# Splitting the last weight row of a memory-bound decode kernel in two: halved loads, products and sums at the very end, and one store of eight pieces

## The chip, the cores and the metric

The kernel runs on one core of one Trainium2 chip. The metric is the device time of one execution in microseconds (us). A profiled execution also leaves a trace; its "span" runs from the first to the last recorded instruction and is 1.2 to 1.4 us shorter than the device time. Times to three decimals below are from the trace's records of instructions, semaphores and DMA packets, which are finer than the views that are printed.

## The reference

A decode step: one token attends to 65536 cached positions, then goes through a mixing block with an MLP, and everything is added up into one row of 1024 numbers. Cut to what the change touches:

```python
# x 1x1x1024, k_cache/v_cache 1x4x65536x128, wq 1024x4096, wo 4096x1024,
# w1, w2 1024x1024, w3 1024x3584, w4 3584x1024, all bf16
def reference(...):
    xn = _layernorm(x)
    ...                                   # attention: o (1x4096); mixing block: x1 (1x1024)
    gh = _gelu(_layernorm(x1) @ w3)       # 1 x 3584
    return x + o @ wo + x1 + gh @ w4      # 1 x 1024
```

The last sum is the whole subject. The product with `w4` is done as 28 "rows": row r pairs the column `gh[:, r]` (one value on each of 128 partitions) with a tile of 128 x 1024 weights, 256 KB.

## The kernel before

`w4` is loaded last of all, by four transfers of 17, 7, 3 and 1 rows. TensorE multiplies each row in four column tiles: the columns 0 to 255 of the result are collected on partition 0, 256 to 511 on partition 32, and so on to partition 96. All 28 rows, the residual and the product with `wo` are added up in one PSUM bank. Then VectorE casts that bank to bf16 and SyncE stores it as four pieces of 512 B.

```python
w4_parts = [(0, 17), (17, 7), (24, 3), (27, 1)]          # first row, rows
def w4_dma(i):                                           # issued by SyncE
    r0, nr = w4_parts[i]
    _dma(q_sp, chan("w4%d" % i), lambda e: e.dma_start(out=KV[:, 2, r0 * D:(r0 + nr) * D], in_=rows_src(B_w4, r0, nr)), writes=[b_W4[i]])

def out_rows(items, reads, last=False):
    fns = []
    for lhs, rhs in items:                               # lhs = gh_bf[:, r:r+1], rhs = row r of w4
        for jj in range(4):
            fns.append(lambda e, lhs=lhs, rhs=rhs, jj=jj: e.matmul(
                S_ps[32 * jj:32 * jj + 1, 0, 0:256], lhs, rhs[:, 256 * jj:256 * jj + 256],
                start=False, stop=last, tile_position=(0, 32 * jj), skip_group_check=True))
    _grp(q_pe, fns, reads=reads, writes=[b_OUT], partial=True)

# ... attention, mixing block; then:
resid_rows()                                             # residual, by products with an identity
wo_rows()                                                # o @ wo, moved into the same bank
for i, (r0, nr) in enumerate(w4_parts):
    out_rows([...], [b_W4[i], b_gh], last=(i == len(w4_parts) - 1))
_op(q_dve, lambda e: e.tensor_copy(orow[:, :], OUT), reads=[b_OUT], writes=[b_orow])      # the CAST
ev_out = _dma(q_sp, chan("out"), lambda e: e.dma_start(out=out[0, 0, :].rearrange("(j n) -> j n", j=4), in_=orow[0:97:32, :]), reads=[b_orow])
q_sp.wait_all([ev_out])
```

`_op`, `_grp` and `_dma` put one instruction, a group of products, or a transfer on an engine's list, and work out from `reads` and `writes` which semaphores it has to wait for.

## Time and profile before

| | before |
|---|---|
| device time, median of 3 runs | 400.3 us |
| bytes read | 169.87 MB at 426 GB/s over the span |
| last w4 row landed | 396.560 |
| its product done (semaphore) | 396.912 |
| CAST | 396.935 to 397.360 |
| store issued by SyncE | 397.388 to 398.021 |
| end of the span | 399.081 |

The upper two lines say that the kernel is bound by its stream of bytes. The others are the tail: what still has to happen once the last byte is there. I call the time from the last landing to the end of the span "the tail": 2.521 us here. The prediction shows the lines of the views that these numbers come from.

### The profile page before, as it was taken

How to read it: one execution, taken by the hardware profiler on the slowest of the kernel's cores; microseconds unless marked ns; L12 is line 12 of the kernel's file. 1: busy time of each engine (PE TensorE's matmuls, PEld its weight loads, DVE VectorE, ACT ScalarE, POOL GpSimd, SP SyncE). 2: the span in 40 equal slices, each digit the busy share in tenths (PEclk: the TensorE clock that was granted, in tenths of full speed). 3: DMA queues.
4: the chain of work that ended last, by engine and by line, in shares of the span. 5: the costliest groups of instructions: out<-in, count | busy, mean ns of one | idle time of the engine just before them, and what ended most of it. 6: DMA issues, size and time to landing. Idle time of an engine off the chain costs nothing.

```text
span 399.1 us, 3429 instructions
## 1 busy us (share of the span) xinstructions
PE 168.9 (42%) x1523; PEld 59.0 (15%) x1484; DVE 221.4 (55%) x260; ACT 23.9 (6%) x50; POOL 7.7 (2%) x31
## 2 busy tenths in 40 slices
PE   0034767338033713460357036413541362137394
PEld 0011334012001210110012001101120110012232
DVE  0024222994298549833984597269647952895201
ACT  1000000011001100110011002000100110011000
POOL 5000000000000000000000000000000000000000
PEclk9998568555655665575557555855585558555969
DMA  9999899999999999999999999999999999999995
GB/s 420 420 388 493 383 441 466 447 415 427 420 427 429 434 460 434 434 427 420 434 427 420 466 440 434 421 420 434 427 427 466 434 440 420 420 427 434 418 414 229
DMA packets 3759, 169.97 MB, mean 426 GB/s; under 512 B 548, under 2 KB 552, under 8 KB 808
## 3 DMA queue, kind: packets, MB, share of 16 engines
q1 hardware_dynamic: 3608, 169.87, 98.7%
q8 instruction: 5, 0.08, 0.1%
q10 hardware_dynamic: 144, 0.00, 0.0%
q14 instruction: 2, 0.02, 0.0%
HBM read 169.87 MB, written 0.00 MB: 426 GB/s over the span
## 4 chain that ended last, share of the span: by engine, by line
DMA 59%; DVE 25%; PE 12%; issue 1%; ACT 1%; SPq 1%; POOL 0%
DMA KV<-in_A_k_cache_dram 45%; DVE KV L460 18%; DMA KV<-in_B_w_dram 8%; DMA KV<-in_A_x_dram 6%; PE S_ps L411 3%; PE OT_ps L518 2%; DVE mrow L481 2%; PE M_ps L426 2%; PE S_ps L474 2%; PE S_ps L379 1%; ACT p_sb L496 1%; DVE Yall L395 1%; DVE pT_f L509 1%; DVE pT_f L419 1%; PE PT_ps L505 0%
## 5 line engine op out<-in xcount | busy, mean ns | idle before, releaser
L460 DVE STREAM_TRANSPOSE KV<-KV 128x4096 f32<-128x4096 f32 x32 | 140.3, 4422 | 44.3 <-DMA KV<-in_A_k_cache_dram 44.3
L474 PE MATMUL S_ps<-KV,Ycur 128*32 128x512 bf16 x512 | 60.7, 624 | 132.5 <-DVE KV L460 132.5
L518 PE MATMUL OT_ps<-KV,pT_f 128*32 128x512 bf16 x512 | 47.2, 511 | 4.0 <-issue 3.0
L474 PEld LDWEIGHTS S_ps<-KV,Ycur 128*32 128x32 bf16 x512 | 14.3, 126 | 160.0 <-DVE KV L460 142.4
L496 ACT ACTIVATE p_sb<-S_ps,brun 128x1024 bf16<-128x1024 f32 x16 | 17.8, 1114 | 276.6 <-DVE brun L494 176.1
L509 DVE STREAM_TRANSPOSE pT_f<-PT_ps 128x512 f32<-128x512 f32 x32 | 22.5, 702 | 14.0 <-PE PT_ps L505 14.0
L481 DVE TENSOR_REDUCE mrow<-S_ps 128x1 f32<-128x1024 f32 x16 | 19.3, 1205 | 11.3 <-PE S_ps L474 11.3
L484 PE MATMUL M_ps<-Rm,Lmat 128*128 128x16 bf16 x16 | 3.1, 194 | 38.0 <-DVE Rm L482 38.0
L529 DVE SCALAR_TENSOR_TENSOR O_acc<-O_acc,ff,OT_ps 128x512 f32<-128x512 f32 x12 | 9.0, 748 | 14.7 <-PE OT_ps L518 14.7
L518 PEld LDWEIGHTS OT_ps<-KV,pT_f 128*32 128x32 bf16 x512 | 13.1, 115 | 23.8 <-issue 16.4
L411 PE MATMUL S_ps<-KV 128*32 128x512 bf16 x88 | 12.1, 538 | 2.7 <-DVE KV L359 2.7
L339 DVE CAST KV<-KV 128x8 f32<-128x8 bf16 x1 | 0.2, 172 | 22.2 <-DMA KV<-in_A_x_dram 22.2
L578 PE MATMUL S_ps<-KV,o_bf 128*1 128x512 bf16 x64 | 9.9, 484 | 4.5 <-DMA KV<-in_A_wo_dram 4.5
L505 PE MATMUL PT_ps<-p_sb,permR 128*128 128x512 bf16 x16 | 9.7, 607 | 0.8
L426 PE MATMUL M_ps<-ident_f,pT_f 64*128 64x2 f32 (+2 forms) x32 | 7.9, 373 | 2.5 <-DVE pT_f L419 2.5
L484 PEld LDWEIGHTS M_ps<-Rm,Lmat 128*128 128x128 bf16 x16 | 1.7, 104 | 49.3 <-DVE Rm L482 49.3
L582 DVE COPY pT_f<-S_ps 1x512 f32<-1x512 f32 x1 | 0.7, 679 | 14.4 <-PE S_ps L578 14.4
L426 PEld LDWEIGHTS M_ps<-ident_f,pT_f 64*128 64x128 f32 (+2 forms) x32 | 7.7, 326 | 4.7 <-DVE pT_f L419 3.1
L419 DVE COPY pT_f<-S_ps 64x512 f32<-64x512 f32 (+1 forms) x3 | 2.1, 685 | 10.8 <-PE S_ps L411 10.8
L505 PEld LDWEIGHTS PT_ps<-p_sb,permR 128*128 128x128 bf16 x32 | 3.3, 102 | 27.5 <-ACT p_sb L496 14.7
L364 PE MATMUL M_ps<-KV 8*128 8x8 bf16 x1 | 0.2, 184 | 16.1 <-DVE Dmat_f L363 16.1
L642 POOL MEMSET pT_f<- 64x512 f32 x1 | 0.5, 520 | 312.4 <-PE OT_ps L518 312.4
(88 smaller groups left out, 90.2 us busy)
## 6 DMA issues: line engine op xcount, KB each, us to landing
KV<-in_B_w_dram SPq DMA_DIRECT2D x1, 7168.0 KB, 48.0
KV<-in_B_w_dram SPq DMA_DIRECT2D x1, 4352.0 KB, 27.4
KV<-in_B_w_dram SPq DMA_DIRECT2D x2, 2048.0 KB, 28.3
KV<-in_B_w_dram SPq DMA_DIRECT2D x1, 1792.0 KB, 31.3
KV<-in_B_w_dram SPq DMA_DIRECT2D x1, 768.0 KB, 32.7
KV<-in_B_w_dram SPq DMA_DIRECT2D x1, 256.0 KB, 32.9
KV<-in_A_k_cache_dram SPq DMA_DIRECT2D x8, 46.7
KV<-in_A_v_cache_dram SPq DMA_DIRECT2D x8, 28.1
```

The costliest lines, as they stand in the source:

```text
L411: fns.append(lambda e, j=j, k=k, mv=mv: e.matmul(S_ps[32 * (k % 4):32 * (k % 4) + 32, bank + k // 4, :], vec[:, j:j + 1].broadcast_to([P, ...
L419: _op(q_dve, lambda e, b=b, nb=nb: e.tensor_copy(pT_f[0:32 * nb, b, :], S_ps[0:32 * nb, bank + b, :]), reads=[b_S[bank + b]], writes=[b_pT ...
L426: fns.append(lambda e, b=b, nb=nb, c=c: e.matmul(M_ps[:, c0 + 16 * b + c:c0 + 16 * b + 4 * nb:4], pT_f[0:32 * nb, b, c:512:4], ident_f[0:3 ...
L460: _op(q_dve, lambda e: e.transpose(out=KV32[:, s, o:o + 4096], in_=KV32[:, s, o:o + 4096]), reads=[b_KV[s][sub]], writes=[b_KV[s][sub]], l ...
L474: fns.append(lambda e, we=we, cm=cm, mv=mv: e.matmul(S_ps[32 * cm:32 * cm + 32, n % 4, :], Ycur[:, we, :, :].rearrange("p a g -> p (a g)") ...
L481: _op(q_dve, lambda e: e.reduce_max(mrow[:, k:k + 1], S_ps[:, 2 * k:2 * k + 2, :].rearrange("p b c -> p (b c)"), axis=AX.X), reads=b_S[2 * ...
L496: _op(q_act, lambda e: e.activation(p_sb[:, :, :].rearrange("p b c -> p (b c)"), S_ps[:, 2 * k:2 * k + 2, :].rearrange("p b c -> p (b c)") ...
L505: _op(q_pe, lambda e: e.matmul(PT_ps[:, :], permR[:, :], p_sb[:, n % 2, :], start=True, stop=True), reads=[b_p[n % 2], b_const], writes=[b ...
L509: _op(q_dve, lambda e: e.transpose(out=pT_f[:, n % 2, :], in_=PT_ps[:, :]), reads=[b_PT], writes=[b_pT[n % 2]], loop=True)
L518: fns.append(lambda e, q=q, q4=q4: e.matmul(OT_ps[32 * q4:32 * q4 + 32, g % 2, :], pT_bf[:, n % 2, q, :, 1], KV[:, s, 8192 * sub + 512 * q ...
L529: _op(q_dve, lambda e: e.scalar_tensor_tensor(out=O_acc[:, 0:512], in0=O_acc[:, 0:512], scalar=ff[:, k:k + 1], in1=OT_ps[:, k, :], op0=ALU ...
L578: _grp(q_pe, [lambda e, j=j, jj=jj: e.matmul(S_ps[32 * jj:32 * jj + 1, 1, :], o_bf[:, j:j + 1], KV[:, 0, j * D + 512 * jj:j * D + 512 * (j ...
```

## The change

The tail is a chain of product, cast and store, each of which waits for all of the one before. The change tries to take half of the first two off it: the last row is loaded in two halves of 512 columns; while the second half is on its way the first is multiplied and added. For that everything else (residual, `wo`, rows 0 to 23) is copied to SBUF ahead of time, rows 24 to 27 are collected in two PSUM banks, one for each half, and VectorE adds bank and copy for 128 columns per partition at a time. The columns of each partition are then not contiguous in the result (two runs of 128), so that the store has eight pieces of 256 B. The products of the second half use weights already in TensorE, so their weight loads are left out. Cut to its core:

```diff
-        orow = sb("orow", [P, 256], BF)
+        orow = sb("orow", [P, 2, 128], BF)
...
-        w4_parts = [(0, 17), (17, 7), (24, 3), (27, 1)]
+        w4_parts = [(0, 17 * D), (17 * D, 24 * D), (24 * D, 27 * D), (27 * D, 27 * D + 512), (27 * D + 512, 28 * D)]
...
+        n_bulk = 2
+        b_half = [b_S[2], b_S[3]]
+        ost = pT_f[:, 1, 0:256]
+        b_ost = b_pT[1]
+        def w4_row(r, jj):
+            return KV[:, 2, r * D:(r + 1) * D].rearrange("p (h j n) -> p j h n", h=2, j=4)[:, jj, :, :]
...                            # out_rows(i): as before, for the loads 0 and 1, columns in the new order
+        def out_halves(r, halves, i, first=False, last=False):
+            def mm(e, hf, jj):
+                f = kept_matmul if halves == (1,) else lambda e, *a: e.matmul(*a[:3], start=first, stop=last, tile_position=a[3], skip_group_check=True)
+                return f(e, S_ps[32 * jj:32 * jj + 1, 2 + hf, 0:128], gh_bf[:, r:r + 1], w4_row(r, jj)[:, hf, :], (0, 32 * jj))
+            _grp(q_pe, [lambda e, hf=hf, jj=jj: mm(e, hf, jj) for hf in halves for jj in range(4)],
+                 reads=[b_W4[i], b_gh], writes=[b_half[hf] for hf in halves], partial=not first)
...                            # residual and wo products: columns in the new order, counts unchanged
-        for i, (r0, nr) in enumerate(w4_parts):
-            out_rows(...)
-        _op(q_dve, lambda e: e.tensor_copy(orow[:, :], OUT), reads=[b_OUT], writes=[b_orow])
-        ev_out = _dma(q_sp, ..., out=out[0, 0, :].rearrange("(j n) -> j n", j=4), in_=orow[0:97:32, :]), reads=[b_orow])
+        for i in range(n_bulk):
+            out_rows(i)
+        _op(q_dve, lambda e: e.tensor_copy(ost, S_ps[:, 0, 0:256]), reads=[b_S[0]], writes=[b_ost])
+        for r in range(24, 27):
+            out_halves(r, (0, 1), 2, first=(r == 24))
+        for hf in range(2):
+            out_halves(27, (hf,), 3 + hf, last=True)
+            _op(q_dve, lambda e, hf=hf: e.tensor_tensor(out=orow[:, hf, :], in0=ost[:, 128 * hf:128 * hf + 128], in1=S_ps[:, 2 + hf, 0:128], op=ALU.add),
+                reads=[b_ost, b_half[hf]], writes=[b_orow], partial=(hf == 1))
+        ev_out = _dma(q_sp, ..., out=out[0, 0, :].rearrange("(h j n) -> j h n", h=2, j=4), in_=orow[0:97:32, :, :]), reads=[b_orow])
```

## The prediction

> **What bounds the kernel now.** I read the page from the top: the slices first, then the chain of waits for the last 40 us, then the timeline of the last 10 us, then single rows of instructions for prices.
>
> ```profile
> span 399.1 us, 3429 instructions
> ...
> DMA  9999899999999999999999999999999999999995
> GB/s 420 420 388 493 383 441 466 447 415 427 420 427 429 434 460 434 434 427 420 434 427 420 466 440 434 421 420 434 427 427 466 434 440 420 420 427 434 418 414 229
> ...
> HBM read 169.87 MB, written 0.00 MB: 426 GB/s over the span
> ```
>
> The DMA row is at 9 in every slice but one and the last: the kernel streams 169.87 MB, and 169.87 MB at 426 GB/s is the span. The change moves no byte less, so it can touch only what follows the stream. The chain of waits shows where that begins:
>
> ```profile
> 363.60 0.04 issue
> 363.64 32.91 DMA KV<-in_B_w_dram
> 396.56 0.04 issue
> 396.60 0.31 PE S_ps L566 x4
> 396.91 0.02 issue
> 396.94 0.42 DVE orow L647
> ```
>
> The last w4 row (256 KB) lands at 396.56. All that the change can win lies between there and 399.1: 2.5 us, 0.6% of the time. The timeline says what PE, DVE and SyncE do there and before it:
>
> ```profile
> 390.83 0.61 PE L584 MATMUL S_ps<-pT_f,ident_f 64*1 64x256 f32 x8 [1.40 <-ACT pT_f L583]
> 391.37 1.73 PEld L566 LDWEIGHTS S_ps<-KV,gh_bf 128*1 128x1 bf16 x68 [0.44 <-issue]
> 391.37 2.03 PE L566 MATMUL S_ps<-KV,gh_bf 128*1 128x256 bf16 x68
> ...
> 394.09 0.93 PE L566 MATMUL S_ps<-KV,gh_bf 128*1 128x256 bf16 x28 [0.69 <-DMA KV<-in_B_w_dram]
> ...
> 395.95 0.50 PE L566 MATMUL S_ps<-KV,gh_bf 128*1 128x256 bf16 x12 [0.93 <-DMA KV<-in_B_w_dram]
> ...
> 396.60 0.28 PE L566 MATMUL S_ps<-KV,gh_bf 128*1 128x256 bf16 x4 [0.15 <-DMA KV<-in_B_w_dram]
> 396.94 0.42 DVE L647 CAST orow<-S_ps 128x256 bf16<-128x256 f32 x1 [6.78 <-PE S_ps L566]
> 397.39 0.63 SPq L648 DMA_DIRECT2D out_dram<-orow  x1
> ```
>
> PE waits for a landing ahead of each of the last three groups (0.69, 0.93, 0.15 us), so the matmuls are not the bound and earlier work has slack. The tail is then: last landing 396.56; product done 396.91; CAST 396.94 to 397.36; store issued 397.39 to 398.02; store landed, end 399.08. The store is the largest piece: 1.7 of the 2.5 us, and the change hurries nothing in it.
>
> For the price of the new DVE sum there is a row of the same kind, one operand in PSUM, one in SBUF, 128 elements, and its successor shows the cost of a wait of DVE on itself (374.14 + 0.28 to 374.46, 34 ns in the instruction records):
>
> ```profile
> 374.14 0.28 DVE L546 TENSOR_TENSOR cb_R<-M_ps,maskD 32x128 f32<-32x128 f32 x1 [1.15 <-PE M_ps L543]
> 374.46 0.37 DVE L549 TENSOR_REDUCE cb_o<-cb_R 32x32 f32<-32x128 f32 x1
> ```
>
> **What the Trainium skill says.** "VectorE: DVE Perf Modes", section on the TRN2 errata: a Vector instruction costs a fixed part of about 150 cycles plus one cycle per element for an fp32 tensor_tensor, at 0.96 GHz. The trace agrees on the fixed part: the CAST of 256 took 425 ns, which is (256+152)/0.96; for 128 elements the page gives 290 ns and the trace 279, which I use. "TensorE: Matmul & The Clock Gate", section "Single matmul latency": (398+N)/2.4 ns at full clock. The trace models the 256-wide products at 270 ns, the page's 272; 128 columns fewer are 53 ns fewer. "DMA: Bandwidth & Descriptors", section on why a DMA increments its semaphore by 16: the number of engines is the largest divisor of the slowest dimension. The packet records agree: four packets of 512 B, for four rows. The new pattern's slowest dimension is still 4, so I expect four engines with two pieces each. The same page, "Specifications": under 512 B a transfer becomes a read-modify-write. No row of before shows what a 256 B write costs.
>
> **The change part by part**, in the order of the tail.
>
> 1. Landing of the last piece. The packet records give 80 ns from packet to packet for 2048 B and 235 for 6144 B, so 0.038 ns per byte and about 3 ns per packet (estimate). Each engine carried 8 packets of 2048 B for the last row; now it carries 8 + 8 of 1024 B at about 41 ns. That is 8 x 3 ns plus one more semaphore write (9 ns): the end moves from 396.56 to about 396.59, +0.03. The first half lands 8 x 41 = 0.33 us before, at about 396.25. The fifth issue of 0.43 us by SyncE at 364 is hidden under 15 us of queued wo transfer.
>
> 2. Product. Before: 0.042 us from landing to start, 0.31 to the semaphore, of which the N-dependent part shrinks by 53 ns. Left out weight loads: four loads of one column start within 10 ns of each other beside the matmuls, so at most 0.01. After: 396.59 + 0.04 + 0.26 = 396.89, against 396.91. Gain 0.02 including the loss of step 1.
>
> 3. DVE. The CAST of 425 ns becomes a sum of 279 ns: -0.146. But it waits for two semaphores, PE's and its own, and where an instruction does so in before (the sum over OT_ps at 371.15) a separate wait of 21 ns stands 66 ns ahead of it. So it starts about 0.09 after the product, not 0.02: +0.066. Starts 396.98, ends 397.26, against 397.36. Gain so far 0.10.
>
> 4. The first sum must be gone by then. First half at 396.25 + 0.04, product to 396.55, wait 0.09, sum 396.64 to 396.92, plus 34 ns for DVE's wait on itself: 396.95. That is 0.03 before 396.98, so it fits, just. The 24 matmuls of rows 24 to 26 start at 395.95 in six groups of four of 55 to 65 ns (a 256-wide group took 104 ns: 2.03 less 0.27, over 17 rows), so are streamed by 396.28 to 396.34, which may hold the first half up by 0.05 and the end by 0.02.
>
> 5. The copy of the bulk from PSUM to SBUF, about 425 ns as the CAST, starts at 395.07, when the second group is done, and ends at 395.50, more than 1 us before use: free. The reordered columns in the residual and wo products keep their counts (16, 64 and 4 matmuls) and lie before waits: free.
>
> 6. Store. Issue 0.63 as now: 128 pieces of a w4 load were issued in 0.33 to 0.43 us, so four more pieces cost next to nothing in issue. On the engine one packet of 29 ns becomes two of about 20: +0.01. The write of 256 B pieces is unpriced: I put 0 to 0.1, middle 0.04.
>
> Sum: -0.02 (steps 1 and 2) - 0.08 (step 3) + 0.01 (step 4) + 0.05 (step 6) = about -0.04; I take 400.3 - 0.05 = 400.25 us.
>
> **The rivals.** (a) The intended gain arrives whole: the first half is off the tail, product and sum are halved, the store costs nothing more: -0.12 at most, 400.18. For it speaks the bare 146 ns between the two DVE rows; against it the doubled wait of step 3. (b) The small pieces spoil the store: read-modify-write on HBM, or a slower issue of a pattern with one more dimension. 1.7 us of the tail is the store, so 20% more would give +0.35: 400.6. For it speaks the skill's limit of 512 B and an issue that already takes 0.63 where loads take 0.33; against it that only four engines and 2 KB are concerned. (c) A wait takes the place of the one removed: rows 24 to 26, now twice as many matmuls, or the first sum, end late, and the second sum queues behind: +0.05 to +0.1 on step 4, 400.3 to 400.35. Step 4 has a margin of 0.03 only, so this is likely in part. (d) Stream: in the records of before five DMA engines reach the last row about 1 us after the other eleven, and 16 KB instruction fetches on single engines stall one for 1 us (378.24 to 379.30). If added PE instructions moved a fetch onto a late engine, the end would move by up to 0.6 us (16 KB at 27 GB/s, from 6144 B in 235 ns). Against: PE's instructions are unchanged up to the last two groups, so the fetches should fall where they did.
>
> **Range and chances.** (a) to (c) span 400.18 to 400.6; three runs of before lie within 0.02. With some room for (d), 8 times in 10: 400.0 to 400.5. Over 2% would be 8 us, three times the whole tail: faster 0.005, within 2% 0.985, slower 0.01.
>
> **What would show it.** In the timeline of after: landing of the last half within 0.1 of 396.59; four 128-wide matmuls with no weight load; two sums of about 280 ns, the second starting 0.07 to 0.12 after its product's end or 34 ns after the first sum; a copy at about 395.07; a store issue near 0.63, and about 1.05 us from its end to the end of the span. I am wrong if the store takes over 1.9 us from issue to end, if the last landing moves by over 0.2, or if the second sum starts over 0.1 after both its producers.

## The result

The changed kernel took 400.35 us (median of 6 fast runs, 400.25 to 400.52); the kernel before took 400.3 us in the same rounds (median of 6, 400.28 to 400.65). The ratio is 1.0, with a 95% interval of 0.9987 to 1.0013. Ratios here and below are the mean time of one kernel's fast runs over that of the other's of the same rounds, so not quite the ratio of the medians quoted. The predicted 400.25 us, range and class hold.

A time that doesn't move says nothing of whether the parts did what they should. The page of the changed kernel shows the same stream as before:

```profile
span 398.9 us, 3478 instructions
...
DMA  9999899999999999999999999999999999999995
```

There are 49 instructions more, and not one slice of the DMA row differs. The timeline of the last 4 us (start and duration in us, engine, line, operation, count, and in brackets what ended the idle time ahead of it):

```profile
394.94 0.42 DVE L677 COPY pT_f<-S_ps 128x256 f32<-128x256 f32 x1 [5.94 <-PE S_ps L586]
...
395.85 0.58 PE L593 MATMUL S_ps<-KV,gh_bf 128*1 128x128 bf16 x28 [0.96 <-DMA KV<-in_B_w_dram]
396.54 0.22 PE L562 MATMUL S_ps<-KV,gh_bf 128*1 128x128 bf16 x4
396.55 0.61 DVE L682 TENSOR_TENSOR orow<-pT_f,S_ps 128x128 bf16<-128x128 f32 x2 [1.19 <-PE S_ps L593]
397.20 0.67 SPq L684 DMA_DIRECT2D out_dram<-orow  x1
```

The copy of the bulk sits 0.9 us ahead of the next landing, harmless. The 28 products are rows 24 to 26 and the first half of row 27. The last four products are half as wide as the four before the change, and no line of weight loads goes with them. The two sums follow each other within one group; the store is issued at 397.20 where it was 397.39. The chain of waits says what the end hangs on (start, duration, what):

```profile
363.05 32.76 DMA KV<-in_B_w_dram
...
395.85 0.61 PE S_ps L593 x28
...
396.55 0.30 DVE orow L682
396.85 0.03 issue
396.88 0.29 DVE orow L682
```

It now ends in sum after sum: it holds that the second sum began when the first was over (396.85 + 0.03), not when the second product was done. That is worth a check, because both could be true at once; the experiments take it up.

Step by step, "after" being this profile:

| us | before | after | difference |
|---|---|---|---|
| last landing | 396.560 | 396.501 | |
| landing to product's semaphore | 0.352 | 0.285 | -0.067 |
| product's semaphore to end of CAST, or of the second sum | 0.448 | 0.382 | -0.066 |
| end of that to start of the store's issue | 0.028 | 0.028 | 0 |
| issue | 0.633 | 0.672 | +0.039 |
| end of issue to end of the span | 1.060 | 1.046 | -0.014 |
| tail: last landing to end | 2.521 | 2.413 | -0.108 |

The tail is 0.11 us shorter, and that is 0.03% of 400 us. Against it stands one loss, which lies ahead of the landing: the time from the last landing of rows 24 to 26 to the last landing of row 27 was 0.654 us before and 0.697 after, +0.043. The same bytes come in twice as many packets, which start 42.3 ns apart on the engine that lands last (80.3 ns for packets of double size), and with one more semaphore to write. This count is too kind to the change, because the landing of rows 24 to 26 comes later too; before_again has a better one.

### The profile page after: what moved, and what is told of

Read it like the earlier page. It is cut to its first block, busy times and chain, and to the rows that moved or that the text cites. A ratio compares the mean times of both kernels' runs of the same rounds, so it can differ in the third digit from the quotient of the medians.

```text
span 398.9 us, 3478 instructions
## 1 busy us (share of the span) xinstructions
PE 176.1 (44%) x1555; PEld 59.5 (15%) x1496; DVE 221.9 (56%) x262; ACT 23.9 (6%) x50; POOL 7.7 (2%) x31
## 4 chain that ended last, share of the span: by engine, by line
DMA 58%; DVE 25%; PE 13%; issue 1%; ACT 1%; SPq 0%; POOL 0%; DVEq 0%
DMA KV<-in_A_k_cache_dram 45%; DVE KV L460 18%; DMA KV<-in_B_w_dram 8%; DMA KV<-in_A_x_dram 6%; PE S_ps L411 3%; PE OT_ps L518 2%; DVE mrow L481 2%; PE M_ps L426 2%; PE S_ps L474 2%; PE S_ps L379 1%; ACT p_sb L496 1%; DVE Yall L395 1%; DVE pT_f L509 1%; PE PT_ps L505 1%; DVE pT_f L419 1%
## 5 line engine op out<-in xcount | busy, mean ns | idle before, releaser
L505 PE MATMUL PT_ps<-p_sb,permR 128*128 128x512 bf16 x32 | 18.6, 581 | 0.8
L606 PE MATMUL S_ps<-KV,o_bf 128*1 128x512 bf16 x64 | 8.8, 442 | 4.6 <-DMA KV<-in_A_wo_dram 4.6
```

What stands on the lines that cost most here:

```text
L505: _op(q_pe, lambda e: e.matmul(PT_ps[:, :], permR[:, :], p_sb[:, n % 2, :], start=True, stop=True), reads=[b_p[n % 2], b_const], writes=[b ...
L606: _grp(q_pe, [lambda e, j=j, jj=jj: e.matmul(S_ps[32 * jj:32 * jj + 1, 1, :].rearrange("p (h n) -> p h n", h=2), o_bf[:, j:j + 1], KV[:, 0 ...
```

## The experiments

Theory: every part does what it was made for and the tail is shorter by 0.11 us, of which the split landing takes back 0.05 to 0.08; the rest, 0.03 to 0.06 us, is below what separates two runs of one kernel. Rivals: the shorter tail is a chance of one profile; the store's small pieces eat the gain; a new wait (sum after sum) eats it. The first six runs take these apart; two price the store, three try to use what they showed, and the last looks at a point that had come up on the way.

### after_again: the changed kernel once more, with five rounds

No edit.

> The changed kernel again, unaltered, to see what is stable and what is run-to-run spread. Main theory (the tail after the last landing is about 0.11 us shorter, and that is lost in the spread of whole runs): last landing of w4 to end of span 2.41 us within 0.03 (before: 2.52), the landing itself anywhere within 0.3 us of 396.5, median time within 0.15 us of before, verdict same. Rival (the stream got slower by the finer pieces and ate the gain): the last landing at least 0.1 us later than the 396.56 of before.

The timeline of this second profile, the line of the two sums:

```profile
396.82 0.62 DVE L682 TENSOR_TENSOR orow<-pT_f,S_ps 128x128 bf16<-128x128 f32 x2 [1.18 <-PE S_ps L593]
```

The tail is 2.418 us (2.413 in the first profile), but everything lies 0.27 us later, because the last landing came at 396.769 in place of 396.501. Timed: 400.59 us (median of 5) against 400.51 us for before (median of 9 in the same rounds), ratio 1.0004 (0.999 to 1.0017). So the tail repeats to 0.005 us, and the landing ahead of it moves by more than twice the gain from one execution to the next. The sign that was set for the rival (a landing 0.1 us later than 396.56) came true as well; the next run shows that it proves nothing, since the kernel before moves as far.

### before_again: the same for the kernel before

No edit, one look.

> The kernel before, unaltered, for a second profile of its tail. Main theory: last landing to end of span 2.52 us within 0.03, so the 0.11 us of difference to the changed kernel (2.41, 2.42) is real and not spread; the landing of the last row within 0.3 us of 396.56, so landings scatter by more than the gain. Rival: the tail itself scatters by 0.1 us, and this one gives anything down to 2.42.

The timeline:

```profile
397.17 0.42 DVE L647 CAST orow<-S_ps 128x256 bf16<-128x256 f32 x1 [7.91 <-PE S_ps L566]
397.63 0.63 SPq L648 DMA_DIRECT2D out_dram<-orow  x1
```

Landing 396.799, tail 2.525 us (2.521). The difference of the tails is 0.108 from the first two profiles and 0.107 from the second two: it is not chance. The landings of before (396.56, 396.80) and after (396.50, 396.77) lie in the same band, and a landing that comes 0.27 us later outweighs a tail that is 0.108 us shorter.

What the split costs ahead of the landing is seen best from a mark that the change doesn't touch: the landing of the last block of `v_cache`, near 360 us. From there to the last landing of `w4` it took 36.510 to 36.523 us in the three profiles with whole rows (before, before_again, two_by_two) and 36.582 to 36.604 in the ten that load as the kernel after does (all other runs but adjacent): a loss of 0.075 us. Counted from the landing of rows 24 to 26 it is smaller, 0.642 to 0.654 against 0.694 to 0.711 in nine of the ten (0.668 in one_row). The packet records have the two parts: the packets of the last row take about 0.04 us longer (from the first one's start to that of the semaphore's write, 0.645 us for the whole row, 0.687 to 0.696 for the halves), and from that last packet to the semaphore it takes 0.501 to 0.506 us in place of 0.474 to 0.476 (0.480 in act_load). Why the second part grew no run shows.

From the same mark to the end of the span it is 39.044 and 39.043 us before, 39.004 and 39.013 after. So the whole change gains about 0.035 us: 0.108 in the tail less 0.075 ahead of it.

### one_bank: halved loads and products, but one bank and one CAST

```diff
-        b_half = [b_S[2], b_S[3]]
+        b_half = [b_S[0], b_S[0]]
-   ... S_ps[32 * jj:32 * jj + 1, 2 + hf, 0:128] ...
+   ... S_ps[32 * jj:32 * jj + 1, 0, 128 * hf:128 * hf + 128] ...
-        (copy to ost, two sums)
+        _op(q_dve, lambda e: e.tensor_copy(orow[...], S_ps[:, 0, 0:256]), reads=[b_S[0]], writes=[b_orow])
```

> The load of the last row in two halves, the halved products and the eight-piece store stay; what goes is the second half of the change: all is summed in one PSUM bank and evacuated by one CAST of 256 elements after the last product. Theory of the working (DVE is the piece that gains: 425 ns with one wait becomes 289 ns with two): last landing to end 0.042 + 0.25 + 0.023 + 0.425 + 0.03 + 1.72 = 2.49 us, 0.07 to 0.08 more than the changed kernel. Rival (the gain is the shorter product and the DVE part nothing): 2.42.

The timeline has narrow last products and one wide CAST:

```profile
396.63 0.22 PE L562 MATMUL S_ps<-KV,gh_bf 128*1 128x128 bf16 x4
396.90 0.42 DVE L681 CAST orow<-S_ps 128x256 bf16<-128x256 f32 x1 [7.92 <-PE S_ps L562]
```

Landing 396.593, end 399.082: a tail of 2.489 us, as expected. One time: 400.42 us. With the VectorE part undone, 0.07 to 0.08 of the 0.11 us are gone (2.489 against 2.413 to 2.418); what stays against before, 0.03, is the narrower product less the dearer store. The two banks, the copy and the sums do earn their share.

### reload: the second half's products load their weights again

```diff
-                f = kept_matmul if halves == (1,) else lambda e, *a: e.matmul(...)
+                f = lambda e, *a: e.matmul(...)
```

> The changed kernel, but the second half's four matmuls load their weights again. Theory (weight loads of one column lie beside the matmuls): landing of the last half to the product's semaphore 0.285 us as now, within 0.01. Rival (left-out loads are part of the gain): 0.02 us or more longer.

In the timeline the weight loads of the last four products are back (PEld is TensorE's weight load):

```profile
396.53 0.09 PEld L593 LDWEIGHTS S_ps<-KV,gh_bf 128*1 128x1 bf16 x4 [0.26 <-DMA KV<-in_B_w_dram]
396.53 0.23 PE L593 MATMUL S_ps<-KV,gh_bf 128*1 128x128 bf16 x4
```

From the landing (396.484) to the product's semaphore it took 0.300 us where the kept weights have 0.285: 0.015 us, halfway between the two expectations, so it decides neither. In its record the first product starts as soon after the landing as with kept weights (0.044 against 0.042 us); where the 0.015 us arise, one profile doesn't show. The tail was 2.442 us. The one time, 400.18 us, is the lowest of that call, with the costlier kernel: a reminder of what single times are worth here.

### one_wait: each sum waits for TensorE alone

The first reading of the chain was that the second sum waits for the first. In the kernel after, each sum carries two waits: for the products, and for VectorE itself. Here each half of `orow` has its own bookkeeping, and a tiny memset waits for the bulk copy long before, so that each sum has the one wait that matters.

```diff
+        _op(q_dve, lambda e: e.memset(mrow[:, 0:1], 0.0), reads=[b_ost], writes=[b_mrow[0]])
...
-                reads=[b_ost, b_half[hf]], writes=[b_orow], partial=(hf == 1))
+                reads=[b_ost, b_half[hf]], writes=[b_orow[hf]])
```

> The two sums no longer wait for DVE itself (two separate marks for the halves of the output row, and a tiny memset takes the wait for the copied bulk early), so each waits for PE alone. Theory that the doubled wait costs 66 ns on the path: the second sum starts 0.02 to 0.04 us after its product's semaphore instead of 0.093, last landing to end of span 2.34 us (0.07 less than the changed kernel). Rival (the second sum was held by the first one's end, not by its waits): it starts no earlier against its product than now, 2.41 us. Whole time: not to be told from before, ratio 1.000 within 0.001.

The second sum started 0.024 us after its product's semaphore in place of 0.093. The tail was 2.394 us, not shorter still, because in this profile the last four products ran at a lower granted clock: the trace models them at 263 ns each, not 216, and their semaphore came 0.333 us after the landing, not 0.285. Timed: 400.34 us (median of 5) against 400.51 for before in the same rounds, ratio 0.9994 (0.998 to 1.0008): a lower median than after_again had in the same rounds (400.59), and still not told apart from before. Its five times (400.26 to 400.45) lie almost wholly under the five of after_again (400.44 to 401.00), but the medians are 0.25 us apart, four times what the tail can give, so most of that is not the two waits.

A later run (act_load, below) has the same sums and fell on the full clock. Its chain of waits:

```profile
396.74 0.04 issue
396.78 0.24 PE S_ps L562 x4
397.02 0.02 issue
397.05 0.29 DVE orow L686
```

The end hangs on the second product again (397.025 by its semaphore, sum from 397.049), and the tail is 2.352 us, 0.06 shorter than after. The first sum of that run was over at 397.011, before the second product was. So in the kernel after the doubled wait is what costs: it puts the first sum's start 0.093 after its product, and with that also the first sum's end where it meets the second one. There the two limits coincide: the second product's semaphore at 396.786 + 0.093 = 396.879, and the first sum's end at 396.843 + 0.035 = 396.878 (0.035 is what such a wait of VectorE on itself took in before, 374.424 to 374.459). The chain of waits can show only one of the two. In after_again they come apart (397.054 + 0.094 = 397.148 against a first sum that ended 0.044 before), and in reload further (its second sum starts 0.093 after its product, 0.058 after the first sum's end), with the doubled wait as the one that binds.

### store_four: the four pieces of before again

The store writes each partition's 256 values as one piece, which puts the columns in a wrong order, so the result is wrong. Everything ahead of it is the kernel after.

```diff
-   out=out[0, 0, :].rearrange("(h j n) -> j h n", h=2, j=4), in_=orow[0:97:32, :, :]
+   out=out[0, 0, :].rearrange("(j n) -> j n", j=4), in_=orow[0:97:32, :, :].rearrange("p h n -> p (h n)")
```

> The changed kernel with the store in four pieces of 512 B as before (the halves then stand in the wrong order in the output: a wrong result on purpose). If eight pieces of 256 B cost what the comparison of the two traces says: issue 0.63 instead of 0.67 us, issue to end of span 1.69 instead of 1.72 us. Rival (small pieces are a read-modify-write that costs more at the receipt): issue to end falls by 0.1 us or more. Rival (no cost, spread only): stays at 1.72.

The timeline, the issue of the store:

```profile
397.27 0.62 SPq L684 DMA_DIRECT2D out_dram<-orow  x1
```

The issue took 0.625 us (0.672 with eight pieces), and from its start to the end of the span it was 1.678 us (1.718). Eight pieces of 256 B cost 0.04 us over four of 512 B, all of it in the issue. The rival that the small writes spoil the store is out.

### store_probe: what does a store of this kernel cost, and what makes it dear?

The store is 1.7 of the 2.4 us of the tail, so it is what a better version should go for. This kernel is the one after with nine more stores of the same 2 KB behind the real one, each waiting for the one before; some write other values of the same size, the last one the row itself, so that the result was right in the end; only the durations count.

```diff
+        for k, (q, (dst, src)) in enumerate([(q_sp, o4), (q_sp, o16), (q_sp, p8), (q_sp, o1), (q_sp, o8), ...]):
+            q.wait_all([ev_out])
+            ev_out = _dma(q, chan("probe%d" % k), lambda e, dst=dst, src=src: e.dma_start(out=dst, in_=src), reads=[...])
```

> After the real store, nine more stores of the same 2 KB, each waiting for the one before, with nothing else on the DMA: SyncE 4 x 512 B, 16 partitions x 128 B, 8 partitions x 256 B, 1 x 2048 B, 8 pieces of 256 B from 4 partitions, 4 x 512 B, 16 x 128 B, then ACT 4 x 512 B and 8 x 256 B. Wrong in between, correct at the end. Issue times by theory that pieces are dear: 0.63, over 0.7, 0.67, 0.6, 0.67. By theory that the issue of a store is dear because the issuing engine writes the semaphore counts of the unused DMA engines: 0.63 for 4 and 1, about 0.33 to 0.4 for 16 partitions, and the whole store shorter by 0.2 us or more with 16. By theory that the landing of a store is fixed: all nine take 1.6 to 1.8 us from issue to the next one's start.

The timeline, four of the nine in order: 4 partitions that lie 32 apart, 16 adjacent partitions, 8 adjacent ones, 1 partition:

```profile
399.16 0.56 SPq L695 DMA_DIRECT2D out_dram<-orow  x1
...
400.80 0.37 SPq L695 DMA_DIRECT2D out_dram<-ident_f  x1
...
402.18 0.31 SPq L695 DMA_DIRECT2D out_dram<-ident_f  x1
...
403.42 0.23 SPq L695 DMA_DIRECT2D out_dram<-KV  x1
```

The second number of each line is the issue; from one start to the next they took 1.639, 1.377, 1.240 and 1.137 us. Sixteen pieces are cheaper than four, so the number of pieces isn't what is dear; one partition, moved by one DMA engine, is the cheapest, so nor is it that few engines take part. The patterns of these kernels, 4 partitions 32 apart, are the dearest (1.619 to 1.657 us in the three that SyncE made here). Theory after this run: the step between partitions is what costs.

### store_probe2: the step between partitions alone

The same again, with patterns that differ in the step only (and single partitions, one after the other).

```diff
+            [(q_sp, row4, orow[0:97:32, :, :]...)],      # 4 partitions, 32 apart
+            [(q_sp, row4, idb[0:4, :])],                 # 4 adjacent
+            [(q_sp, row4, idb[0:7:2, :])],               # 4, two apart
+            [(q_sp, row2, KV[0:33:32, 2, 0:512])],       # 2 partitions, 32 apart
+            [(q_sp, row2, KV[0:2, 2, 0:512])],           # 2 adjacent
...
```

> Nine more store steps after the real one, each waiting for the one before: 4 partitions 32 apart (512 B each), 4 adjacent, 4 two apart, 2 that are 32 apart (1 KB each), 2 adjacent, then 4 single-partition stores of 512 B one behind the other, the same from the output row in two pieces each, 4 adjacent from ACT, and two singles each from SyncE and ACT. First theory (the step between partitions is what made the 4-partition stores dear, 0.55 us of issue against 0.31 for 8 adjacent ones): 0.55, 0.3, 0.55, over 0.45, 0.28. Second theory (the number of DMA engines, 4, decides): 0.55 for all three of 4, under 0.3 for both of 2. Four singles: 0.23 each, all landed 0.9 us after the last one's issue began to end, so 1.75 to 1.85 in all, no gain on SyncE alone; two and two: about 1.4 if ACT's issues run beside SyncE's, 1.8 if not.

The timeline, the first four patterns of the edit in order:

```profile
399.18 0.58 SPq L711 DMA_DIRECT2D out_dram<-orow  x1
...
400.84 0.31 SPq L711 DMA_DIRECT2D out_dram<-ident_f  x1
...
402.04 0.62 SPq L711 DMA_DIRECT2D out_dram<-ident_f  x1
...
403.75 0.50 SPq L711 DMA_DIRECT2D out_dram<-KV  x1
```

Four partitions cost 0.58 us to issue when they lie 32 apart, 0.62 two apart, 0.31 side by side; from start to next start 1.656, 1.704 and 1.205 us. Two cost 0.50 and 0.26. Any step over one brings the cost, whatever its size, so it isn't the distance. A single partition with one piece took 0.23 to 0.25, a single one with two pieces 0.56 to 0.62. So a store from adjacent partitions would save about 0.45 us of the tail. Why the issuing engine takes longer for such patterns no run shows. The two guesses on several stores at once missed: four single ones by SyncE took 2.03 us to the start of the next store (1.75 to 1.85 expected), and two each by SyncE and ScalarE, of two pieces each, 2.64 us to the last landing (1.4 or 1.8).

### adjacent: the result on eight adjacent partitions

To have the last result side by side, rows 21 to 27 are multiplied with weights padded by zeros, so that product c of a row lands on partition c of eight; the sums of the rest are moved from partitions 0, 32, 64, 96 to those eight by two small transfers issued by ScalarE's queue. Rows 21 to 26 are loaded one by one, to keep the serial products short.

```diff
+        n_col = 21
+        w4_parts = [(0, 17 * D), (17 * D, n_col * D)] + [(r * D, (r + 1) * D) for r in range(n_col, 27)] + [(27 * D, 27 * D + 512), (27 * D + 512, 28 * D)]
...
+                S_ps[0:8, 2, 0:128], gh15[:, c // D - n_col, 7 - (c % D) // 128:15 - (c % D) // 128], KV[:, 2, c:c + 128],
...
+            _dma(q_act, chan("ost%d" % hf), lambda e, hf=hf: e.dma_start(out=ost8[4 * hf:4 * hf + 4, :], in_=ost[0:97:32, 128 * hf:128 * hf + 128]), ...)
...
+        ev_out = _dma(q_sp, ..., out=out[0, 0, :].rearrange("(q n) -> q n", q=8), in_=orow8[0:8, :], ...)
```

> A version built from what the store probes showed: the result stands on 8 adjacent partitions, 256 B each, so that the store is the 8-adjacent form (1.24 us in the probe against 1.64 to 1.66 for the strided ones). Rows 0 to 20 are summed as in the changed kernel, copied to SBUF and moved to the 8 partitions by two small transfers that ACT issues 4 us before the end; rows 21 to 27 come in loads of one row (the last in two halves), with 8 products of 128 columns each into one tile, one after the other instead of four at a time; one sum of 128 elements, with its transfer waits taken early, then the store. Theory: from the last landing: 0.04 + 4 products one after the other 0.21 to 0.32 + 0.22 to the semaphore + 0.02 + 0.29 sum + 0.03 + store 1.24 to 1.35 = 2.1 to 2.25 us to the end, against 2.41 of the changed kernel and 2.52 of before; the whole 0.2 to 0.4 us under before, ratio 0.9990 to 0.9995, verdict same. Rival: the serial products of rows 21 to 27 fall behind the stream (over 0.64 us per row) or the moved sums come late, and the end is as late as now or later; the landing may also be 0.05 us later for the finer loads.

The timeline, the one sum on eight partitions and the store:

```profile
397.73 0.28 DVE L693 TENSOR_TENSOR orow<-pT_f,S_ps 8x128 bf16<-8x128 f32 x1
398.03 0.37 SPq L694 DMA_DIRECT2D out_dram<-orow  x1
```

The tail shrank more than expected, to 2.030 us, with the store at 1.232 us from start to end, as the probe had it. The time did not: 400.87 us (median of 5) against 400.51, ratio 1.0008 (0.9995 to 1.0022). The landing came at 397.233, later than in any other run. The loads of one row landed 0.66 us apart (mean of six), where the loads of seven and three rows in after_again took 0.62 us per row; from the landing of rows 0 to 16 to that of row 26 it took 6.540 us against 6.204, with five loads more. The moved sums landed at 397.602, so late that the sum began 0.048 us after its product and not 0.024. From the mark near 360 us to the end of the span it is 38.974 us, which is 0.03 less than after: inside the span the cheaper store paid for the finer loads, and little more. But the time outside the span was 1.56 to 1.69 us (mean 1.62, before 1.27), where before, after and one_wait have 1.21 to 1.44, and that is about the whole difference of the medians.

### two_by_two: the kernel before with four single-partition stores from two queues

```diff
-        ev_out = _dma(q_sp, chan("out"), ... in_=orow[0:97:32, :]), reads=[b_orow])
+        ev_out = [_dma((q_act, q_sp)[j % 2], chan("out%d" % j), lambda e, j=j: e.dma_start(out=out[0, 0, :].rearrange("(j n) -> j n", j=4)[j:j + 1, :], in_=orow[32 * j:32 * j + 1, :]),
+                       reads=[b_orow]) for j in range(4)]
```

> The kernel before, with one thing altered: its one store of four rows that lie 32 partitions apart becomes four stores of one partition and 512 B each, two issued by SyncE and two by ACT at the same moment. Theory from the probes (a store from one partition is issued in 0.23 to 0.26 us, one from partitions 32 apart in 0.55 to 0.63; the landing follows 0.85 to 0.9 us after the issue ends): end of the CAST to end of span 0.03 + 0.26 + 0.04 + 0.26 + 0.87 = 1.45 us instead of 1.72, last landing to end 2.25 us instead of 2.52 of before and 2.41 of the changed kernel; the whole 0.2 to 0.3 us under before, ratio about 0.9993. Rival (ACT's first issue after a long pause is slow, 1.11 us in one probe, 0.54 in another, or the two engines' issues exclude each other): 1.7 us or more from the CAST's end, no gain.

The timeline, two issues on each engine:

```profile
397.61 0.62 SPq L648 DMA_DIRECT2D out_dram<-orow  x2
397.62 0.76 ACTq L648 DMA_DIRECT2D out_dram<-orow  x2
```

The two issues of SyncE took 0.62 us together and those of ScalarE 0.76, where the one issue of before took 0.633: the issues save nothing. The first issue of ScalarE alone took 0.49 us. By the packet records the four pieces started at 398.350, 398.382, 398.702 and 398.854; which DMA engines carried them the records don't say. The tail was 2.580 us, 0.06 longer than before. Of that, 0.085 is the wait at the end, which is for four semaphores in two steps and not for one (0.119 us from the last piece's landing to the end of the span, 0.034 before); to the last piece's landing the store is 0.03 us faster than before. The time outside the span was 1.57 to 1.74. Timed: 401.02 us against 400.63, ratio 1.0012 (0.9999 to 1.0026). The rival for this run (no gain) holds.

### one_row: everything on one partition

All rows are collected in two banks from the start, in 128-column products; at the end VectorE and ScalarE copy the eight pieces (four each) to one partition, from which one piece of 2048 B is stored.

```diff
-   (products of 256 columns into one bank for rows 0 to 23, copy to ost, two sums)
+   (products of 128 columns into two banks for all rows)
+   for jj in 0..3 of each half: tensor_copy (jj < 2, VectorE) or activation Copy (ScalarE) of S_ps[32 * jj:32 * jj + 1, 2 + hf, 0:128] into one partition
+   ev_out = _dma(q_sp, ..., out=out[0, 0, :].rearrange("(j n) -> j n", j=1), in_=KV[0:1, 1, 0:D], reads=b_row)
```

> A second version built on the store probes, with no transfer issued by ACT: the whole result is brought to one partition, whose store of one piece of 2048 B took 1.14 us in the probe. Everything is summed in the two PSUM banks of the halves from the start (no copy ahead, no sums on DVE); each half is evacuated by four copies of 128 elements into one partition, two by DVE and two by ACT, the first half's while the second lands; then one store by SyncE. Theory: last landing to the product's semaphore 0.285; DVE's and ACT's copies follow each other at about 0.2 us, four of them from 0.04 before the landing to 0.85 after it; two waits of SyncE 0.08; store 1.14 to 1.25: last landing to end 2.1 to 2.2 us, against 2.41 of the changed kernel and 2.52 of before; the landing itself as in the changed kernel; time 400.2 to 400.4, ratio about 0.9993. Rival: the copies in a row cost what the store gains, 2.4 us or more.

The timeline of TensorE and VectorE:

```profile
394.16 0.45 PE L586 MATMUL S_ps<-KV,gh_bf 128*1 128x128 bf16 x20 [0.73 <-DMA KV<-in_B_w_dram]
396.93 1.01 PE L586 MATMUL S_ps<-KV,gh_bf 128*1 128x128 bf16 x60 [2.33 <-issue]
...
398.05 1.22 DVE L683 CAST KV<-S_ps 1x128 bf16<-1x128 f32 x4 [7.91 <-PE S_ps L562]
```

The store is short, 1.198 us from start to end. But TensorE stood still for 2.33 us from 394.61, and the view finds nothing that it waited for ("issue"). Over that stretch, from 394.44 to 395.54, the records have a fetch of 16,384 B by the queue that brings instructions; in the kernels before and after such a fetch takes 0.9 to 1.1 us, and the last one (from 394.28 and 393.98) begins beside the 28 products of rows 17 to 23, which go on undisturbed, and ends in the wait for the next landing. This kernel has 1643 TensorE instructions for 1555 after. That the fetch stopped it is my reading from the times, not proved by a run, and before and after show that TensorE can work on beside a fetch; nor does the fetch alone account for the second half of the pause. On top, four copies of 0.28 us follow one another with 0.31 from start to start, 1.2 us where the one sum takes 0.29. Tail 3.856 us, 401.75 us against 400.45, ratio 1.0025 (1.0011 to 1.0039): slower by a quarter of a per cent, and the only run whose interval lies off 1.

### act_load: does a transfer issued by ScalarE cost time outside the span?

adjacent, two_by_two and both probes have ScalarE issue transfers late, and have 0.35 to 0.53 us more outside the span than before (means; the probes ran once each). Here one_wait gets a single load of 2 KB on ScalarE's queue in the middle of the kernel, where it can delay nothing.

```diff
+            if m == 3:
+                _dma(q_act, chan("xa"), lambda e: e.dma_start(out=orow[:, 0, 0:8], in_=A_x[0, 0, :].rearrange("(p j) -> p j", p=P)), writes=[b_xa])
```

> The one-wait version once more, with one addition in the middle of the kernel: ACT issues a 2 KB load that nothing needs (into 16 B per partition of the output row's place). Two separate questions. First, the tail: with the PE clock at full, last landing to end of span 2.34 us within 0.03 (the first profile of it gave 2.39 with the last four matmuls at a lower clock); rival: 2.39 or more again. Second, the part of the measured time that lies outside the span: 1.2 to 1.4 us in all kernels so far except those in which ACT issued a transfer after its first one at the start, where it was 1.6 to 1.7. Theory (any later transfer by ACT costs this, wherever it stands): 1.55 to 1.75 here in all runs, so the time is about 0.35 us over the one-wait version. Rival (it is the transfer near the end that costs): 1.2 to 1.4.

Outside the span: 1.45 to 1.55 us, mean 1.48, against a mean of 1.32 for before. That is +0.16, between what the two theories asked for, so the cause stays open: a transfer of ScalarE early on goes with less than what the late ones go with. Timed: 400.8 us against 400.39, ratio 1.0007 (0.9993 to 1.0021). The tail, 2.352 us, is the one quoted under one_wait.

## Why the prediction was right, point by point

The time, the range and the class hold, and so does the reason: only the end could change, and the tail is 0.6% of the time. That the time fell into a range of 0.5 us is in part luck: the range took "three runs of before lie within 0.02" for the spread, but later the kernel before alone had medians of 400.39 to 400.63, and the 400.59 of after_again would have missed it. By the steps:

1. **Landing.** Predicted +0.03; measured +0.075 from the mark near 360 us (before_again). This is the term that was sized too small. The packets were nearly right: they start 42.3 ns apart, against the 41 that was estimated from packets of 2048 and 6144 B, and cost about 0.04 us in all. What was left out is the 0.03 us more from the last packet to the semaphore. The first half landed 0.340 ahead of the second (predicted 0.33). The sign of being wrong "if the last landing moves by over 0.2" was too tight: it moved by 0.24 between two profiles of the kernel before.
2. **Product.** Predicted -0.05 by itself; measured -0.067. The kept weights, put at 0.01 at most, are worth about 0.015 (reload, one profile).
3. **VectorE.** Predicted -0.08; measured -0.066. The start 0.09 after the product was right (0.093). The sum took 289 ns, not 279: the formula of the Trainium skill ("VectorE: DVE Perf Modes", section on the TRN2 errata) gave 290, and I chose a row of the trace with 32 partitions instead. In adjacent the same sum on 8 partitions took 276 ns, so the number of partitions is the likely reason for the 10 ns; no run varied it alone.
4. **The first sum fits, just.** It did: both limits of the second sum fell within 0.001 us of 396.879 in the profiled run. Rival (c), that this wait would cost 0.05 to 0.1, is out: removing the doubled wait gains 0.06 (act_load), but that part was already in step 3.
5. **Copy of the bulk.** Predicted from 395.07, measured from 394.94: free, as said.
6. **Store.** Predicted +0.05 with a range to 0.1; measured +0.025 between the two kernels and 0.04 in store_four. The issue, which was said to be the same, is what grew (0.633 to 0.672); the part after the issue, where the read-modify-write of small pieces was feared, did not grow (1.060 to 1.046).

The sum was -0.04 (the text then takes -0.05, and for rival (b) 400.6 where 400.3 + 0.35 is 400.65) and is 0.075 - 0.067 - 0.066 + 0.025 = -0.033; measured as a whole it is about -0.035 (before_again). That the sum fits so well is luck too: the landing was off by +0.045, and product, VectorE and store by -0.017, +0.014 and -0.025, and the 0.01 of step 4 did not come. Rival (a), the whole gain, is ruled out by the landing and by the doubled wait; rival (b) by store_four; rival (d), a fetch of instructions on a late DMA engine, did not show in after (five fetches of 16 KB as before, the last from 393.98, before from 394.28), though one_row may have met such a fetch on TensorE's side. What no timing here can show is the -0.035 us itself: the 95% interval of the ratio, 0.0013 to either side, is 0.5 us.

## What to carry to other kernels

When a kernel is bound by its stream, read the chain behind the last landing first: its length caps what any change of the end can bring, and here 2.5 us of 400 settled the class before any detail. Judge such a change in the profile, from a landing that it doesn't touch to the end of the span, which repeats to 0.01 us, and not by the time, which moves by several tenths; the tail alone repeats to 0.005 us but leaves out what the change costs ahead of it, here 0.075 of 0.108 us. And take the largest piece of the tail first, but price what its cure adds elsewhere: of three ways to a cheaper store, adjacent and one_row had it and lost the gain to finer loads and time outside the span, or to a pause of TensorE and copies in a row, and two_by_two hardly had it at all.

## What the Trainium skill lacked or had wrong

- "DMA: Bandwidth & Descriptors" has no price of an issue by pattern. Here SyncE took 0.26 to 0.31 us for 2 to 8 adjacent partitions, 0.50 to 0.62 for 2 or 4 partitions with any step over one, 0.23 to 0.25 for one partition in one piece and 0.56 to 0.62 in two, in the probes; at the end of a kernel it was 0.37 for 8 adjacent partitions, 0.32 for one, and 0.63 to 0.72 for 4 that lie 32 apart. The whole 2 KB store took 1.14 to 1.24 us in the cheap forms (1.33 to 1.38 for 16 adjacent partitions) and 1.57 to 1.70 in the strided ones.
- The same page, "Specifications", has 512 B as the least size for the full rate, with a read-modify-write below. For eight pieces of 256 B that cost nothing that could be seen after the issue: 1.046 us from its end to the end of the span, against 1.060 with 512 B. The page doesn't say how little it weighs in a store of 2 KB.
- No page that I read prices a load more on the same queue: cutting 256 KB in two moved the last landing by 0.075 us.
- "VectorE: DVE Perf Modes" prices an instruction (289 ns measured, 290 by the page) but not its start: 0.024 us after the semaphore with one wait, 0.093 with two, 0.035 after an instruction of its own engine that it waits for.
- "Runtime: NRT & Kernel Launch", section "Instruction fetch mechanics", calls the crossing of a 16 KiB block mostly hidden. The fetches took 0.9 to 1.1 us in before and after, and in one_row TensorE stood for 2.33 us around one (that the fetch was the cause is argued, not proved).
- No page that I read has the time outside the span that goes with transfers issued by ScalarE: 0.16 us for one early load, 0.35 to 0.53 with late ones; the cause is open.
